# A chunked delta-rule scan and two MoE layers on one core: a rebuilt opening, and the second half backwards

## The chip, the core and the metric

The kernel runs on one core of a Trainium2 chip (trn2). Its time is device time in microseconds, from the first to the last instruction and what lies around them; lower is better. Engines are named as in the profile: PE (TensorE's matmuls) and PEld (its weight loads), DVE (VectorE), ACT (ScalarE), POOL (GpSimd), SP (which only issues DMAs here).

## What is computed

A scan with the delta rule over 768 steps for 4 x 8 heads of 48, a gated MoE layer of 384 by 2048, and a soft-routed MoE layer of 8 experts. Cut to what matters:

```python
# q, k, v: (4, 8, 768, 48) f32, beta: (4, 8, 768)
k_n = k / (norm(k) + 1e-06)
for t in range(768):
    y[t] = q[t] @ state
    state = state + beta[t] * outer(k_n[t], v[t] - k_n[t] @ state)
x = y.reshape(3072, 384)
h = x @ w_in                        # 384 x 2048, w_in and w_out are float64
x = (h * sigmoid(h)) @ w_out        # 2048 x 384
P = exp(x @ w_gate - max)           # 3072 x 8
for _ in range(8):
    P /= P.sum(1) + 1e-09
    P /= P.sum(0) + 1e-09
    P *= 3072 / 8
out = sum(P[:, e:e+1] * (relu(x @ w1[e]) @ w2[e]) for e in range(8))   # 384 x 1024 x 384
```

## The kernel before

Products are made from a high and a low part in fp32r (hh, hl, lh), so every operand is split in two beforehand: high part by ScalarE's copy, low part by a subtraction.

**Phase 1** runs to about 780 us. The scan goes in 12 steps s of 64 positions. Of each step the key grams `gk` (one for each of two batch pairs bp) are multiplied on PE (`gram_k`), negated into `gneg` by ACT, written to DRAM (`nd`), and read back as `nu`, one 32 x 32 matrix on a partition; one `nu` holds two steps, j = s // 2. `tri(j)` inverts it on DVE: a root and scale chain on 128 x 32 values, one multiplication of `nu`, then 31 columns of 118 short operations on `tmpu` and `tu`, and a last multiplication. ACT copies the result to `nu`, which goes through DRAM (`rd`, `td`) into `rt` and `td11`. `merge` joins the halves (z, r), and the chain of a step on PE, ACT and DVE is c (state read), d, y (output) and s (state), t (transposition) and `x1`. For each block of 256 tokens follow, for 8 values of p, h (18 matmuls of 128x256) with the gate g, and x2p (18 matmuls). These are the bulk of PE's work in phase 1. The weights of this layer are float64 in DRAM: `weight()` takes each of 32 tiles of 128x384 to high and low part: ACT takes the absolute value, POOL bounds it (`guard`), DVE makes four passes (L806, L817, L819, L812), ACT copies the high part, and the low part is the residual, for the first `NPE` tiles by PE (`wp`: three matmuls and an ACT copy), for the others by POOL in two operations (L849, L852).

**Phase 2** is two halves m of 1536 tokens with 32 units n each. A unit has 15 products p (three matmuls of 128x512) from weights `wa`, sums by DVE, POOL and ACT (`room`, `h`), and 12 outputs o (six of 128x384) with `wb`, added to `acc`. POOL and ACT prepare `wa` and `wb` of the next unit (`weights`), and `tokens(m)` prepares the tokens of a half.

What order each engine runs in is settled by a list scheduler (`Order`): operations are added with an engine, a cost, dependencies, a priority and pools (`take`), and it emits, by modelled times, the ready one with the highest priority. `IDLE` and `pe()` are part of its model of PE: while PE would wait it fills in dummy matmuls (`idle`). `FIRST` raises the priority of the first step's chain. Costs, priorities and pool sizes are numbers written by hand, so a new number moves rows on every engine.

Of the kernel before, what the change touches and what calls it, by code (L numbers as in the profile page):

```python
# [33 lines left out]
NPE = 13  # L34
IDLE = 30
# [6 lines left out]
FIRST = 2  # L42
# [156 lines left out]
def kernel(  # L199
# [72 lines left out]
    sc = Order({"a": 3, "m": 2, "x": 1, "wy": 3, "sg": 3, "g": 2, "x1": 2, "stg": 4, "wt": 3, "wp": 3, "ke": 2, "gneg": 1,  # L272
# [30 lines left out]
    def load_kv(s, prio):  # L303
# [8 lines left out]
    def load_k(s, bp, prio):  # L312
# [5 lines left out]
        x = op("SP", 0.27, lambda: go(0), prio=prio, take=["ke"])  # L318
        return [x, op("SP", 0.27, lambda: go(1), [(x, -9.0)], prio=prio)]

    def gram_k(s, bp):
# [21 lines left out]
        e = O["gn", s, bp] = op("ACT", 0.48, ev, [m], prio=4.5)
        sc.free(m, "a", [e])
        if bp == 0:
            O["gm", s] = m
            return
        es = [O["gn", s, 0], e]
        j, hf = s // 2, s % 2
        w = []  # L350

        def put(q):
            if q == 0 and hf == 0:
                T["nd", j] = dram.tile([128, 1024], F32, tag="nd", bufs=2, name=f"nd{j}")
            g = T["gneg", s].rearrange("p b h c -> p (b h) c")
            c0, r0 = 32 * (q % 2), 64 * hf + 16 * q
            nc.sync.dma_start(out=T["nd", j][r0:r0 + 16].rearrange("u (r c) -> r u c", c=32),
                              in_=g[32 * q:32 * q + 32, :, c0:c0 + 32])
# [1030 lines left out]
```

## Time and profile before

| | |
|---|---|
| runs, us | 2299.9, 2299.54, 2294.35 (median 2299.54) |
| profiled execution, us | 2295.31, span 2293.5 |
| granted PE clock, mean over the span | 0.976 |
| busy PE, DVE, ACT, POOL | 96%, 77%, 45%, 72% |
| chain that ended last, by engine | PE 77%, DVE 12%, POOL 2% |
| forty slices of 57 us, PE's busy tenths | 6, 6, 7, 8, then 9 to the end |

The shares are averages over stages with different limits. Of the forty slices only the first four are not full on PE, and the granted clock reads 8, 7, 7 and 9 tenths there.

### The profile page before, as it was taken

Reading aid. Unit: us, or ns where it says so; the run is one execution under the profiler, and the core shown is the slowest. Engines: PE = TensorE matmul, PEld = TensorE weight load, DVE = VectorE, ACT = ScalarE, POOL = GpSimd, SP = SyncE. Lnnn points to the kernel's source line nnn. Section 1 sums busy time; section 2 is a strip of 40 time slices with the busy share of each in tenths; the row PEclk is TensorE's granted clock in tenths of the full one; section 3 lists DMA queues with packets and bytes.
Section 4 is the critical chain, followed back from the end, with each engine's and each line's share of the span. In section 5 each row is a group of like instructions: output and inputs, shape, how many; then the busy total and the mean of one; then the engine's idle time right before and its main releaser. Section 6 shows DMA issues by size and latency. Waiting matters only on the chain.

```text
span 2293.5 us, 43638 instructions
## 1 busy us (share of the span) xinstructions
PE 2198.0 (96%) x17378; PEld 2018.9 (88%) x17378; DVE 1767.2 (77%) x2975; ACT 1030.8 (45%) x1794; POOL 1655.5 (72%) x1480
## 2 busy tenths in 40 slices
PE   6678999999999899999999999999999999999999
PEld 5578988999999788999998999988999999999998
DVE  6997777453223788888888888897888888888887
ACT  4433333333334545545454545455445454545453
POOL 5577543433436788898888888897888888888884
PEclk8779999999999999999999999999999999999999
DMA  8523432222102101010101111111111111010101
GB/s 215 150 69 91 100 80 75 66 70 60 45 14 77 70 28 35 28 42 28 42 28 35 35 35 35 35 56 49 35 35 35 35 30 40 28 42 28 42 28 49
DMA packets 121837, 121.78 MB, mean 53 GB/s; under 512 B 82657, under 2 KB 90593, under 8 KB 121633
## 3 DMA queue, kind: packets, MB, share of 16 engines
q1 hardware_dynamic: 121632, 118.99, 18.2%
q8 instruction: 136, 2.23, 0.4%
q14 instruction: 69, 0.56, 0.1%
HBM read 100.09 MB, written 18.87 MB: 52 GB/s over the span
## 4 chain that ended last, share of the span: by engine, by line
PE 77%; DVE 12%; POOL 2%; issue 1%; ACT 1%; DMA 1%; SPq 0%; DVEq 0%; POOLq 0%; ACTq 0%
PE o L1242 33%; PE p L1156 27%; PE h L673 6%; PE x2p L714 6%; DVE tu L488 3%; DVE tmpu L490 2%; DVE s L971 2%; DVE sg L682 1%; DVE room L971 1%; PE d L596 1%; PE y L611 1%; PE c L577 1%; DMA kqp<-in_kq 0%; DVE wr L817 0%; PE s L627 0%
## 5 line engine op out<-in xcount | busy, mean ns | idle before, releaser
L1156 PE MATMUL p<-room,wa 128*128 128x512 f32 x2880 | 738.4, 396 | 4.6 <-DVE s L971 2.8
L1156 PEld LDWEIGHTS p<-room,wa 128*128 128x128 f32 x2880 | 537.0, 188 | 103.9 <-ACT wa L1063 3.2
L1242 PE MATMUL o<-wb,room 128*128 128x384 f32 x2784 | 603.0, 338 | 8.9 <-POOL room L971 3.6
L971 DVE TENSOR_TENSOR s<-s,p 128x512 f32<-128x512 f32 x704 | 476.1, 684 | 154.2 <-ACT s L1170 61.7
L1242 PEld LDWEIGHTS o<-wb,room 128*128 128x128 f32 x2784 | 500.2, 188 | 28.4 <-POOL room L971 4.6
L971 POOL TENSOR_TENSOR room<-s,room 128x512 fp32r<-128x512 f32 x232 | 319.9, 1379 | 226.5 <-ACT s L1189 174.8
L1258 DVE SCALAR_TENSOR_TENSOR acc<-o,pr,acc 128x384 f32<-128x384 f32 x708 | 421.4, 612 | 46.1 <-PE o L1242 42.4
L1242 PE MATMUL o<-wb,h 128*128 128x384 f32 x1824 | 419.3, 338 | 4.5 <-DVE sm L1312 3.1
L1242 PEld LDWEIGHTS o<-wb,h 128*128 128x128 f32 x1824 | 329.2, 188 | 24.3 <-DVE sm L1312 3.7
L971 POOL TENSOR_TENSOR wa<-wraw,wa 128x640 fp32r<-128x640 f32 x192 | 327.8, 1720 | 0.6 <-ACT wa L1063 0.6
L1187 ACT ACTIVATE room<-s 128x512 fp32r<-128x512 f32 x232 | 145.6, 628 | 385.6 <-DVE s L971 385.6
L971 POOL TENSOR_TENSOR wraw<-wraw 128x256 f32<-128x256 f32 (+2 forms) x384 | 280.9, 752 | 15.1 <-DMA wraw<-in_w 5.4
L690 POOL TENSOR_TENSOR g<-sg,g 128x512 fp32r<-128x512 f32 x96 | 128.4, 1338 | 214.6 <-ACT g L686 214.1
L1189 ACT ACTIVATE s<-s 128x512 f32<-128x512 f32 x384 | 243.1, 633 | 12.2
L1063 ACT ACTIVATE wa<-wraw 128x640 fp32r<-128x640 f32 x192 | 140.8, 734 | 234.0 <-POOL wraw L971 223.6
L714 PE MATMUL x2p<-g,w 128*128 128x256 f32 x1728 | 234.9, 291 | 7.5 <-POOL g L690 5.8
L673 PE MATMUL h<-x,w 128*128 128x256 f32 x1728 | 229.4, 289 | 5.5 <-DVE sg L682 5.5
L714 PEld LDWEIGHTS x2p<-g,w 128*128 128x128 f32 x1728 | 218.8, 196 | 12.5 <-POOL g L690 7.2
L971 DVE TENSOR_TENSOR s<-p,s 128x512 f32<-128x512 f32 x320 | 218.9, 684 | 7.2 <-PE p L1156 2.7
L673 PEld LDWEIGHTS h<-x,w 128*128 128x128 f32 x1728 | 216.1, 194 | 8.7 <-DVE sg L682 6.3
L971 POOL TENSOR_TENSOR h<-s,h 128x512 fp32r<-128x512 f32 x152 | 209.0, 1375 | 10.2 <-ACT s L1189 10.0
L971 DVE TENSOR_TENSOR s<-s,s 128x512 f32<-128x512 f32 x192 | 202.7, 1056 | 2.3
(163 smaller groups left out, 2342.2 us busy)
## 6 DMA issues: line engine op xcount, KB each, us to landing
wraw<-in_w SPq DMA_DIRECT2D x128, 384.0 KB, 3.1
kv<-in_kv SPq DMA_DIRECT2D x12, 768.0 KB, 4.9
kqp<-in_kq SPq DMA_DIRECT2D x40, 192.0 KB, 3.5
wr<-in_w_in SPq DMA_DIRECT2D x16, 384.0 KB, 5.3
wr<-in_w_out SPq DMA_DIRECT2D x16, 384.0 KB, 4.4
x2d<-xr SPq DMA_DIRECT2D x36, 128.0 KB, 1.7
xraw<-x2d SPq DMA_DIRECT2D x6, 768.0 KB, 7.5
out<-acc SPq DMA_DIRECT2D x24, 192.0 KB, 1.9
```

Of the source, the lines that this page charges most:

```text
L488: nc.vector.tensor_tensor(out=tu[:, a:b, 0:k], in0=tu[:, a:b, 0:k], in1=tv, op=ALU.add)
L490: nc.vector.tensor_tensor(out=tv, in0=nu[:, a:b, t:k].to_broadcast([128, b - a, k]), in1=tu[:, t:k, 0:k].to_broadcast([128, b - a, k]), op ...
L673: nc.tensor.matmul(out=ps[:, i], lhsT=w[:, k, wl], rhs=x[:, k, xl], start=n == 0, stop=n == 8)
L690: nc.gpsimd.tensor_tensor(out=g[:, 1], in0=T["sg", b, p], in1=f32(g)[:, 0], op=ALU.subtract)
L714: nc.tensor.matmul(out=T["x2p", b][j], lhsT=w[:, wl, 128 * j:128 * j + 128], rhs=g[:, gl, i], start=p == 0 and n == 0, stop=p == NP - 1 an ...
L971: e.tensor_tensor(out=out, in0=in0, in1=in1, op=o)
L1063: nc.scalar.activation(P2[key][:, :, 0], R(3 + 5 * g, 8 + 5 * g), AF.Copy)
L1156: nc.tensor.matmul(out=ps, lhsT=w[:, i, wl], rhs=x[:, xl], start=k == 0, stop=k == 2)
L1187: nc.scalar.activation(P2[key][:, 0], buf(x), AF.Relu)
L1189: op2("ACT", 0.52, lambda: nc.scalar.activation(buf(x), buf(x), AF.Relu), writes=[("s", n, x)], prio=PR_H)
L1242: nc.tensor.matmul(out=ps, lhsT=h[:, hl, 128 * i:128 * i + 128], rhs=w[:, wl], start=c == 0, stop=c == 5)
L1258: op2("DVE", 0.53, lambda A=A, pk=pk, t=t: nc.vector.scalar_tensor_tensor(out=A(), in0=P2[pk], scalar=P2["pr"][:, t, e:e + 1], in1=A(), op ...
```

## The change

In the opening: the key loads, grams and `nd` writes of steps 0 and 1 get priority 30; two loads each of step 1 and some of the reads of `nu` and `rt` are issued by ACT. `nd` is now written per step in its natural layout (two contiguous writes) and `units(j)` reads it into `nu` in eight scattered reads; `gl` is gone. The gram q·k of the first two steps, its mask, the square and reduction of the norms wait for the first inverse or move from POOL to DVE and ACT. `weight()` converts two tiles in one instruction for 24 of the 32 tiles; the guard moves from POOL to DVE, and PE makes all 32 residuals, those from the ninth on in a pool shared with the other matmuls. `NPE`, `IDLE`, `FIRST`, pool sizes and costs are changed. In phase 2 the second half takes its units from the last to the first, so that unit 32 uses unit 31's `wa` and `wb`, and no preparation stands between. By count PE has 57 matmuls of residuals and 57 idle ones more; POOL has 93 fewer operations.

```diff
-NPE = 13
-IDLE = 30
+NPE = 8
+IDLE = 0.9
-FIRST = 2
+FIRST = [20, 5] + [0] * 10
-    sc = Order({"a": 3, "m": 2, "x": 1, "wy": 3, "sg": 3, "g": 2, "x1": 2, "stg": 4, "wt": 3, "wp": 3, "ke": 2, "gneg": 1,
+    sc = Order({"a": 3, "m": 2, "x": 1, "wy": 3, "sg": 3, "g": 2, "x1": 2, "stg": 3, "wl": 2, "wp": 3, "ke": 2, "gneg": 1,
...
         def ev():
+            if s < 2 and bp:
+                nc.vector.tensor_scalar(out=T["gneg", s][:, bp], in0=T["gk", s, bp], scalar1=-1.0, scalar2=None, op0=ALU.mult)
+            else:
...
+        def put():
+            if bp == 0:
+                T["nd", s] = dram.tile([128, 16, CH], F32, name=f"nd{s}")
+            nc.sync.dma_start(out=T["nd", s][:, 8 * bp:8 * bp + 8], in_=T["gneg", s][:, bp])
+    def units(j):
...
+        for s in (2 * j, 2 * j + 1):
+            for q in range(4):
...
+                by = "ACT" if s == 1 and q % 2 else "SP"
...
+                    (nc.scalar if by == "ACT" else nc.sync).dma_start(
+                        out=nu[r0:r0 + 16], in_=T["nd", s][32 * q:32 * q + 32, :, c0:c0 + 32].rearrange("r u c -> u r c"))
...
-        m = op("PE", 1.26, pe, O["ld", s][bp] + ([O["gn", 3, 1]] if s < 2 else []), prio=5, take=["a"], turn=1)
+        m = op("PE", 1.26, pe, O["ld", s][bp] + ([O["td2", 0]] if s < 2 else []), prio=5 if s < 2 or s > 3 else 1.5, take=["a"], turn=1)
-        if s < 2:
-            e = [op("ACT", 0.48, lambda p=p, b=b: nc.scalar.activation(t[p, b], T["gq", s, bp][p], AF.Copy), [m], prio=-8)
-                 for p, b in at]
-            O["pm", s, bp] = [op("POOL", 1.25, lambda p=p, b=b: nc.gpsimd.tensor_tensor(
-                out=t[p, b], in0=t[p, b], in1=mask[p].unsqueeze(1).to_broadcast([64, H, CH]), op=ALU.mult),
-                [x, O["mask"]], prio=5.5) for x, (p, b) in zip(e, at)]
+        e = O["pm", s, bp] = [op("DVE", 0.6, lambda p=p, b=b: ev(p, b), [m, O["mask"]], prio=31) for p, b in at]
...
-    def weight(kind, f):
+    def weight(kind, f, m):
...
-            nc.gpsimd.tensor_scalar(out=T["wm", n], in0=T["wm", n], scalar1=TINY_HI, scalar2=None, op0=ALU.max)
+            v.tensor_scalar(out=t(), in0=t(), scalar1=TINY_HI, scalar2=None, op0=ALU.max)
...
         def rest():
-            ps = T["wp", n] = psX.tile([128, 512], F32, tag=f"x{n % 3}", name=f"wp{n}")[:, 0:DM]
+            if n < NPE:
+                ps = T["wp", n] = psX.tile([128, 512], F32, tag=f"x{n % 3}", name=f"wp{n}")[:, 0:DM]
+            else:
+                ps = T["wp", n] = psA.tile([128, 512], F32, tag="a", name=f"wp{n}")[:, 0:DM]
...
-        def rest_pool():
-            nc.gpsimd.tensor_tensor(out=view(f32(t())), in0=view(f32(hw())), in1=f32(part(0)), op=ALU.subtract)
...
-        def lo_pool():
-            nc.gpsimd.tensor_tensor(out=part(1), in0=view(f32(t())), in1=view(f32(lw())), op=ALU.add)
...
-    keys(0, 13.5)
-    keys(1, 6)
+    keys(0, 30)
+    keys(1, 30)
+    units(0)
...
-            for f in range(2 * p, 2 * p + 2):
-                weight(kind, f)
+            for f in range(2 * p, 2 * p + 2, 2 if p < NP - 2 else 1):
+                weight(kind, f, 2 if p < NP - 2 else 1)
...
+    def wn(n):
...
+        return NQ - 1 if n == NQ else n
...
+    def at(n):
+        return (0, n) if n < NQ else (1, 2 * NQ - 1 - n)
...
     for n in range(2 * NQ + 1):
-        if n + 1 < 2 * NQ:
-            weights((n + 1) % NQ, n + 1)
+        if n + 1 < 2 * NQ and n + 1 != NQ:
+            weights(at(n + 1)[1], n + 1)
```

How rows move, at four places. First VectorE from where it waits for `nu` (L419 and L417 are the same line of the root chain); `wt` and `wr` are tiles of a weight. Before:

```order
L419 TENSOR_SCALAR rta<-nu 128x32
L806 TENSOR_SCALAR wt_342<-wm_311 128x384
L817 SCALAR_TENSOR_TENSOR wr_251<-wr_251,wt_342 128x384
L819 TENSOR_SCALAR wt_342<-wr_251 128x384
L812 SCALAR_TENSOR_TENSOR wl_352<-wr_251,wt_342 128x384
L415 RECIPROCAL rta<-du 128x32
L416 TENSOR_TENSOR rta<-rta 128x32
```

After:

```order
L919 TENSOR_TENSOR wgr<-wgs,wgr 128x3x8
L417 TENSOR_SCALAR rta<-nu 128x32
L413 RECIPROCAL rta<-du 128x32
L414 TENSOR_TENSOR rta<-rta 128x32
L415 TENSOR_TENSOR rta<-rta,du 128x32
L416 TENSOR_SCALAR du<-rta 128x32
```

A whole weight tile stood between the wait and the root chain, and none stands there now. On GpSimd, from the norms of step 1 to the refill of `tu` (L461), which comes behind the first inverse, the order was:

```order
L802 TENSOR_SCALAR wm_523<-wm_523 128x384
L434 TENSOR_TENSOR sq_1_562<-kv_370 128x384
L442 TENSOR_TENSOR kv_370<-kv_370,ne_518 128x384 x2
L401 TENSOR_TENSOR kqp_84<-kqp_84,mask 64x512 x2
L401 TENSOR_TENSOR kqp_85<-kqp_85,mask 64x512 x2
L401 TENSOR_TENSOR kqp_86<-kqp_86,mask 64x512 x2
L401 TENSOR_TENSOR kqp_87<-kqp_87,mask 64x512 x2
```

and now, from the opening's last memsets:

```order
L288 MEMSET kqp_86 32x512
L288 MEMSET kqp_87 32x512
L463 MEMSET tu 128x1024
L464 MEMSET tu 128x32
L443 ISA
L443 TENSOR_TENSOR kv_353<-kv_353,ne_427 128x384
```

The guards, squares and mask multiplications are gone from there; the first `kv` waits for norms that wait for the first inverse. Third, TensorE between the first products and the merge of step 2. Before, at the third and fourth h of the first block (`d` is the scan's):

```order
L714 MATMUL x2p_0_1620<-g_1_1614,w_344 128x256 x6
L714 MATMUL x2p_1_1621<-g_1_1614,w_344 128x256 x6
L714 MATMUL x2p_2_1622<-g_1_1614,w_344 128x256 x6
L673 MATMUL h_2_1721<-x_0_1342,w_882 128x256 x18
L596 MATMUL d_0_1749<-wq_0_1686,rt 64x48 x16
L673 MATMUL h_3_1772<-x_0_1342,w_1031 128x256 x18
```

After, behind the fifth x2p of the first block:

```order
L721 MATMUL x2p_0_1577<-g_4_2077,w_1942 128x256 x6
L721 MATMUL x2p_1_1578<-g_4_2077,w_1942 128x256 x6
L721 MATMUL x2p_2_1579<-g_4_2077,w_1942 128x256 x6
L872 MATMUL wp_2133<-wr_1728,ident 128x384
L873 MATMUL wp_2133<-w_2104,nident 128x384
L874 MATMUL wp_2133<-wl_2043,nident 128x384
L872 MATMUL wp_2139<-wr_1728,ident 128x384
L873 MATMUL wp_2139<-w_2104,nident 128x384
L874 MATMUL wp_2139<-wl_2099,nident 128x384
```

Residuals of weights, three matmuls each, now stand between the products. Last, GpSimd at the turn of the halves. Before:

```order
L971 TENSOR_TENSOR room_10143<-s_9397,room_10143 128x512
L971 TENSOR_TENSOR h_10153<-s_9398,h_10153 128x512
L971 TENSOR_TENSOR wb_10092<-wraw_9384,wb_10092 128x384
L971 TENSOR_TENSOR wb_10096<-wraw_9384,wb_10096 128x384
L971 TENSOR_TENSOR wraw<-wraw 128x256
L971 TENSOR_TENSOR wraw<-wraw 128x128
L971 TENSOR_TENSOR wraw<-wraw 128x256 x2
L971 TENSOR_TENSOR wraw<-wraw 128x384
L971 TENSOR_TENSOR wraw<-wraw 128x256
L971 TENSOR_TENSOR wa_9385<-wraw,wa_9385 128x5x128
L971 TENSOR_TENSOR wa_9386<-wraw,wa_9386 128x5x128
```

After, the corresponding rows (numbers of names are shifted by one):

```order
L984 TENSOR_TENSOR xt_9391<-xraw 128x512
L984 TENSOR_TENSOR h_10157<-s_9397,h_10157 128x512
L984 TENSOR_TENSOR room_10144<-s_9398,room_10144 128x512
L984 TENSOR_TENSOR wb_10093<-wraw_9385,wb_10093 128x384
L984 TENSOR_TENSOR h_10154<-s_9399,h_10154 128x512
L984 TENSOR_TENSOR wb_10097<-wraw_9385,wb_10097 128x384
L984 TENSOR_TENSOR room_10000<-xraw,room_10000 128x512
L984 TENSOR_TENSOR xraw<-xraw 128x512
L984 TENSOR_TENSOR wa_9387<-wraw,wa_9387 128x5x128
```

The second pass over `wraw` with its `wa` between those `wb` and the tokens' `room` and `xraw` is gone.

## Rows read from the trace of the kernel before

**Rows 1.** The page: busy line of all engines; then a line of its DMA issues.

```profile
PE 2198.0 (96%) x17378; PEld 2018.9 (88%) x17378; DVE 1767.2 (77%) x2975; ACT 1030.8 (45%) x1794; POOL 1655.5 (72%) x1480
...
kqp<-in_kq SPq DMA_DIRECT2D x40, 192.0 KB, 3.5
```

**Rows 2.** Windows: stretch, length, busy PE PEld DVE ACT POOL, granted clock, DMA share, GB/s.

```profile
120.00:140.00 20.00, 15.34 (x242) 14.12 (x243) 19.56 (x36) 9.41 (x17) 13.24 (x12) 0.75 0.27 83
140.00:160.00 20.00, 15.33 (x175) 14.46 (x175) 19.64 (x32) 4.94 (x10) 13.99 (x13) 0.76 0.09 14
160.00:300.00 140.00, 131.72 (x1952) 125.11 (x1951) 105.66 (x205) 51.47 (x93) 87.21 (x84) 0.96 0.36 90
```

**Rows 3.** Timeline (start, us, engine, line, operation, idle before): nu and the first inverse.

```profile
25.51 0.34 SPq L380 DMA_DIRECT2D nu<-nd  x1
...
30.21 0.26 DVE L419 TENSOR_SCALAR rta<-nu 128x32 f32<-128x32 f32 x1 [0.80 <-DMA nu<-nd]
...
34.34 1.75 DVE L480 TENSOR_TENSOR nu<-nu,du 128x1024 f32<-128x1024 f32 x1
...
37.34 0.26 DVE L490 TENSOR_TENSOR tmpu<-nu,tu 128x16 f32<-128x16 f32 x2
...
75.94 1.23 DVE L503 TENSOR_TENSOR tu<-tu,du 128x1024 f32<-128x1024 f32 x1
```

**Rows 4.** Timeline: columns of the first inverse on DVE, and GpSimd beside them.

```profile
55.03 1.54 DVE L490 TENSOR_TENSOR tmpu<-nu,tu 128x91 f32<-128x91 f32 x2
...
63.89 1.55 DVE L490 TENSOR_TENSOR tmpu<-nu,tu 128x64 f32<-128x64 f32 x2
...
65.37 0.48 DVE L488 TENSOR_TENSOR tu<-tu,tmpu 128x64 f32<-128x64 f32 x2
...
53.67 11.43 POOL L401 TENSOR_TENSOR kqp<-kqp,mask 64x512 f32<-64x512 f32 x8
```

**Rows 5.** Timeline of PE: from the first merge z to h, and z of step 2.

```profile
87.33 1.53 PE L545 MATMUL z<-rt,td 32*32 32x32 f32 x64 [0.45 <-DMA rt<-rd]
...
101.46 0.42 PE L611 MATMUL y<-xs,kqp 112*64 112x48 f32 x2 [4.35 <-ACT xs L601]
...
114.41 0.31 PE L611 MATMUL y<-xs,kqp 112*64 112x48 f32 x1 [5.27 <-DVE xs L632]
...
122.38 0.90 PE L644 MATMUL t<-ident,y 128*128 128x128 f32 x3 [4.57 <-ACT y L616]
...
125.06 4.34 PE L673 MATMUL h<-x,w 128*128 128x256 f32 x18
...
209.12 1.20 PE L545 MATMUL z<-rt,td 32*32 32x32 f32 x64
```

**Rows 6.** Timeline of PE: a residual, a key gram, and one h.

```profile
88.80 0.94 PE L841 MATMUL wp<-wr,ident 128*128 128x384 f32 x2
...
90.02 0.27 PE L332 MATMUL gk<-ke 48*64 48x64 f32 x1
...
91.09 0.94 PE L841 MATMUL wp<-wr,ident 128*128 128x384 f32 x2
...
233.82 2.42 PE L673 MATMUL h<-x,w 128*128 128x256 f32 x18
```

**Rows 7.** Timeline of DVE: the first operations of two successive weight tiles.

```profile
77.09 0.35 DVE L806 TENSOR_SCALAR wt<-wm 128x384 int32<-128x384 int32 x1
...
79.01 0.35 DVE L806 TENSOR_SCALAR wt<-wm 128x384 int32<-128x384 int32 x1
```

**Rows 8.** Groups by line and shape, POOL, 80 to 300 us.

```profile
L849 POOL TENSOR_TENSOR wt<-wr,w 128x384 f32<-128x384 f32 x19 | 21.2, 1117 | 10.4 <-ACT w L836 8.2 <-ACT sg L678 2.2
```

**Rows 9.** Windows of a middle stretch and the turn; POOL's groups, 1515 to 1562 us.

```profile
1000.00:1200.00 200.00, 200.00 (x1012) 182.09 (x1011) 173.15 (x270) 97.03 (x165) 169.06 (x147) 1.00 0.11 34
1520.00:1540.00 20.00, 14.93 (x72) 12.36 (x72) 19.72 (x26) 11.87 (x21) 19.84 (x17) 0.99 0.23 80
1540.00:1560.00 20.00, 16.42 (x71) 13.69 (x72) 18.03 (x25) 8.16 (x14) 18.80 (x14) 0.92 0.28 98
...
L971 POOL TENSOR_TENSOR wa<-wraw,wa 128x640 fp32r<-128x640 f32 x6 | 10.2, 1712 | 0.0
```

More of the change, by code (lines that the diff above doesn't have):

```diff
@@ L122, in pe @@
     def pe(self, t, cost, cols):
+        slow = 2 if cols > 768 or cols == 256 else 1.5
         left = 1.0
@@ L126, in pe @@
             k = int(t / self.TICK + 1e-6)
-            c = cost if self.cols.get(k - 1, 0) >= self.FULL else 2 * cost
+            c = cost if self.cols.get(k - 1, 0) >= self.FULL else slow * cost
             x = min(left, ((k + 1) * self.TICK - t) / c)
@@ L298, in load_part @@
         t = kqp[(2 * s + bp) % 4]
-        after = [(O["nl", 0], -1.0), O["z", 2 * s + bp]] if part else []
+        after = [(x, -1.0) for x in O["nl", 0]] + [O["z", 2 * s + bp]] if part else []
+        if s and not part:
+            return [(op("ACT", 0.45, adma(t[64:112, 0], kq[s, bp, 0, :, 0]), prio=prio), 2.3),
+                    (op("ACT", 0.45, adma(t[0:48, 0], kq[s, bp, 1, :, 0]), prio=prio), 2.3)]
         return [op("SP", 0.27, dma(t[64:112, part], kq[s, bp, 0, :, part]), after, prio=prio),
@@ L347, in gram_k @@
             return
[L348 to L358, printed above, removed]
@@ L858, in weight @@
-        a = op("SP", 1.09, ld, free, prio=-9 if n >= 3 else 9.2, take=[] if n < 2 * NF - 1 else ["x1"])
-        ab = O["wabs", n] = op("ACT", 0.41, absolute, [a], prio=-4, take=["stg"])
-        x = op("POOL", 1.14, guard, [ab], prio=-3.5)
-        xs_ = []
-        for c, fn in parts:
-            take = ["wt"] if fn is shift else ["sg"] if fn is tail and n < NPE else []
-            x = op("DVE", c, fn, [(x, 0.13)], prio=1.5, take=take, turn=0)
-            xs_.append(x)
-        sc.free(ab, "stg", [xs_[0]])
@@ L867, in weight @@
-        before = [O["whi", n - 1], O["wlo", n - 1]] if n else []
-        h = O["whi", n] = op("ACT", 0.41, hi, [xs_[1]] + before, prio=7.5)
-        if n < NPE:
-            sc.free(xs_[0], "wt", [x])
-            x = op("PE", 0.97, rest, [x, h, O["ident"], O["nident"]], prio=11, take=["wp"], turn=0, cols=1536)
-            sc.free(xs_[3], "sg", [x])
-            l = op("ACT", 0.41, lo, [x], prio=19.5)
-            sc.free(x, "wp", [l])
+        if p == NP - 1:
+            before = [O["whi", n - 1], O["wlo", n - 1]]
+        elif i:
+            before = [(O["whi", n - 1], 0.0)]
+        else:
+            before = [O["wlo", m] for m in range(max(0, n - 4), n)]
```

230 lines of the change are left out of this document (124 added, 106 removed).

## The prediction

> **What bounds the kernel now.** I first read the busy shares and the forty slices. TensorE is busy 96% of the span [rows 1], and its slices read 9 from the fifth on: away from the start the kernel is bound by TensorE's matmuls, and only a stretch in which TensorE stands, or runs at a low granted clock, can give time back. So I went on with the windows of 20 us. The start is such a stretch: from 120 to 160 us TensorE is busy 15.3 of each 20 us at a granted clock of 0.75, while VectorE is busy 19.6 [rows 2]. Busy share times clock is what TensorE did of what it could: 0.58 there, 0.90 from 160 to 300 (131.72 of 140 at 0.96). I call this the yield. The only other one that the change touches is the turn from the first half of the products to the second, at 1520 to 1560, below.
>
> The timeline of the start then shows who is waited for. The matrix nu, on which the first inverse works, was issued at 25.51 and VectorE waited for it until 30.21; the multiplication that follows stands at 34.34, the first column of the inverse at 37.34, and its last multiplication ends at 77.2 [rows 3]. Behind it come ScalarE's copy, rd, rt and the first merge z at 87.33, and from there one long serial chain, in which TensorE waits 4.35, 5.27 and 4.57 us for results of ScalarE and VectorE, to the first product h at 125.06 [rows 5]. Only from there is there bulk work.
>
> **The change part by part.**
>
> *Keys first.* Loads, key grams, evictions, nd and nu now stand at the head of their queues. A key load takes 3.5 us to land [rows 1], nu took 4.7 us from issue to its first reader [rows 3]. Issue at 1.2, keys of the second step some 2 us later on ScalarE's queue: landed by 6.9; four grams at 1.07 us [rows 6] while others arrive, 10; eviction 0.6; nd written at a load's 3.5, 14.1; nu at 4.7, 18.8. The eight scattered reads in place of one contiguous one are not shown before; at 0.36 us of issue for six in a row on SP I add 0.7: 19.5. Bounds: 17 (evictions overlap) and 24 (the 1.6 MB of weights issued ahead of nd, and the two conversions that stand before nu on VectorE, come in between).
>
> *GpSimd still.* From the root to the first column VectorE took 7.1 us (30.21 to 37.34), in which one weight tile and the norms' reductions lie; by the order these are gone, 4.0 remain. The columns took 38.6 us (37.34 to 75.94). While GpSimd made its eight mask multiplications (53.67, 11.43 us), a pair of 128x91 took 1.54 us; a pair of 128x64 took 1.55 while they ran and 0.48 right behind them [rows 4]. In the new order GpSimd has nothing but memsets until the inverse is through. From 65.37 to 75.94, with GpSimd still, 58 of the 118 column operations took 10.57 us [rows 3, 4]; at that rate all take an estimated 21.5. With the last multiplication of 1.2: end at 19.5 + 4.0 + 21.5 + 1.2 = 46.2, where it was 77.2.
>
> The Trainium skill (SBUF — State Buffer, "Who interferes with whom") has a reason for these rows: a VectorE instruction with two inputs in SBUF and a GpSimd one that reads SBUF lock each other out for a whole instruction. Rows 4 agree in which operations stretch. The rule also speaks against the change: pairs of weight tiles make VectorE's instructions nearly twice as long, and GpSimd's halves of g, some fourteen until the third merge, would each wait up to 0.5 us more (a tile's 1.92 us over four passes); that estimate, 7 us, stands in no term of the sum.
>
> *First chains favoured.* From the inverse's end to z were 10.1 us (77.2 to 87.33), to h a further 37.7. Half of the latter is conversions placed between, and two of three waits are for results that VectorE or ScalarE made late. Behind the inverse the new order gives VectorE fifty rows before h: some 24 us of work, with four mask pairs and nearly four pairs of tiles among it. So h comes 24 to 26 us behind the inverse, if rt lands as before: 46 + 25 = 71 (bounds 65 and 80) in place of 125.
>
> *Weights two at a time, all residuals on TensorE.* This is not free: 19 tiles more get their low word from TensorE at 1.22 us each (88.80 to 90.02 [rows 6]), 23 us of new work. It is in the following count. What it saves is GpSimd's: 19 times 1.1 us [rows 8], twice, and the guards, which go to VectorE. VectorE's 1.92 us for a tile [rows 7] becomes about the same with the guard (one more operation, but four fixed costs halved): nothing either way.
>
> *The count to the third merge.* From h to the z of step 2, the new order of TensorE holds 15 h and 12 x2p of 18 matmuls each (2.42 us, both 128x256 [rows 6]): 65.3; 28 residuals, 34.2; 10 key grams, 10.7; 18 short pieces of the scan at about 1 us, 18. Together 128 us. At a yield of 0.58 (120 to 160 before) this takes 221 us, at 0.90 142, at 0.95 135. I take 0.92, so 139: TensorE has about twice the work of before in this stretch, VectorE less than before, and GpSimd's conversions are gone. The end is at 71 + 139 = 210, where z of step 2 was at 209.1 [rows 5]. At that point the new kernel is ahead, by the two orders, by 12 key grams, 3 h and 5 x2p: 12.8 + 19.4 = 32 us that TensorE, the bound of everything after, need not do later. Opening: 32 - 1 = **31 us** gained, 36 at a yield of 0.95, 10 at 0.80.
>
> *Second half backwards.* Its first unit is the last of the first half, so its weights are there and one unit's preparation on GpSimd falls away, with its loads. At the turn TensorE is busy 14.93 of 20 us at 0.99 and then 16.42 at 0.92, where it is busy 200 of 200 elsewhere: 14.8 and 15.1 of 20, so some 10 us lost. GpSimd is full there, 19.84 and 18.80; the first pass over wa alone is 5.1 us for a unit (six for two units, 10.2) [rows 9], and wb and wraw come on top. But VectorE is at 19.72 as well, with the new tokens. I take 7 of the 10; bounds 0 and 10. What is late next is VectorE's s and room.
>
> The rest (Sqrt table early, Square on ScalarE, put_low gone, 57 more idle matmuls, which fill holes before the first z) has its cover: ScalarE is busy 45% and the idle matmuls stand ahead of waits. I cost it at nothing; without cover the idle ones are 57 x 0.13 = 7 us, in the first 45 us only.
>
> **Sum.** The profiled execution is 2295.3 us: 2295.3 - 31 - 7 = 2257. The median of three runs (2299.5) lies 4.2 above it, so 2261 against the runs (the forecast).
>
> **The rivals.**
>
> 1. *The conversion throttles the products.* A tile passes VectorE, ScalarE, TensorE and ScalarE again, with two buffers for the low words and three for the pairs, and each product of the first token block waits for its tile. With the yield at 0.78 the stretch takes 164 us, the opening gains 6 us, the time is 2287. For: VectorE was full from 120 to 160 [rows 2]. Against: TensorE gets other blocks' h and key grams in between.
>
> 2. *Slower: TensorE starves and its clock stays down.* The same place, the mechanism that the rows from 120 to 160 show already: TensorE waits for a full VectorE, its busy share sinks, the granted clock is 0.75, and everything takes longer. Now 34 us of residuals lie in that stretch, which it didn't hold before. It decides below a yield of 0.72 (128/0.72 = 178; 71 + 178 = 249, about 209 + 32 + 7). At 0.65 it is 2320, at the 0.58 of before 2343. Against: the ratio of TensorE's work to VectorE's is much higher than it was there.
>
> 3. *The turn doesn't gain.* VectorE at 19.72 of 20 is the real bound there, and a still GpSimd changes nothing, so the change doesn't do there what it says: 2269.
>
> 4. *More.* Rows of 1.22 us for a residual and 2.42 for a product contain pieces at a low clock and overlapping; if the true work is a tenth less (13 us) and done at 0.95, the opening gives 49, the turn 10: 2240.
>
> **How the numbers follow.** Forecast (yield 0.83 to 0.95, turn 3 to 10): 0.55, 2253 to 2281. Rival 1: 0.20, a quarter of it within 0.3% of no change. Rival 2: 0.09, some 0.02 of it within 0.3%. Rival 3: 0.10. Rival 4: 0.06. A measurement can tell about 0.3% (7 us) from no change. Faster: 0.55 + 0.15 + 0.10 + 0.06 = 0.86; same 0.05 + 0.02 = 0.07; slower 0.07. The range leaves out half of rival 4 and the slow end of rivals 1 and 2: 2238 to 2292. Predicted is the forecast, 2261.
>
> **What would show it.** In the profile after: nu lands at 17 to 24; the column pairs of the first inverse take under 0.6 us all through; its last multiplication ends at 43 to 50; first h at 65 to 80; the windows from there to the third merge show TensorE's busy share times clock near 0.9; z of step 2 at 200 to 225; the turn shows no weight preparation on GpSimd and less idle on TensorE. I am wrong if the inverse still ends behind 60 (nu late, or its operations stretched by something else than GpSimd), if the yield behind h is that of 120 to 160 before, or if phases between 300 and 1500, which the change hardly touches, get longer and give the lead back.

## The result, and the profile after

The changed kernel takes 2311.21 us (median of 4 runs, 2308.43 to 2312.69) where the kernel before, in the runs beside it, takes 2298.09 (2294.35 to 2299.9): ratio 1.0055, 95% interval 1.004 to 1.0069. It is some 13 us slower; 2261 was predicted, and 2292 was the upper end of the range. The profiled execution is 2310.37 us with a span of 2308.6, 15.1 more than the 2293.5 of before.

The page's busy line, to be set beside [rows 1]:

```profile
PE 2223.4 (96%) x17506; PEld 2036.2 (88%) x17506; DVE 1746.3 (76%) x2971; ACT 1030.6 (45%) x1792; POOL 1543.7 (67%) x1387
```

GpSimd lost 112 us of work, as meant. TensorE got 25 us more: the residuals that had been GpSimd's low words, and the new idle matmuls. It is still busy 96%.

**The start.** The timeline of the kernel after (start, length, engine, line, operation, idle time before it and what ended it), to be set beside [rows 3 to 5]:

```profile
25.07 0.19 DVE L417 TENSOR_SCALAR rta<-nu 128x32 f32<-128x32 f32 x1 [5.19 <-DMA ke<-in_kq]
...
28.78 0.27 DVE L493 TENSOR_TENSOR tmpu<-nu,tu 128x16 f32<-128x16 f32 x2
...
36.11 0.47 DVE L493 TENSOR_TENSOR tmpu<-nu,tu 128x91 f32<-128x91 f32 x2
...
49.47 1.23 DVE L506 TENSOR_TENSOR tu<-tu,du 128x1024 f32<-128x1024 f32 x1
...
65.78 1.92 PE L552 MATMUL z<-rt,td 32*32 32x32 f32 x64 [4.84 <-DMA rt<-rd]
...
85.75 3.54 PE L680 MATMUL h<-x,w 128*128 128x256 f32 x18
...
231.24 1.51 PE L552 MATMUL z<-rt,td 32*32 32x32 f32 x64
```

The first inverse ends at 50.7 where it ended at 77.2, and the first product starts at 85.75 where it started at 125.06. Up to there the kernel is 39 us ahead. But the merge of step 2, at 231.24, is 22 us behind the 209.12 of before. The reads of nu and VectorE between 164 and 224 show why:

```profile
164.40 3.50 SPq L384 DMA_DIRECT2D nu<-nd  x4
...
177.71 0.19 DVE L417 TENSOR_SCALAR rta<-nu 128x32 f32<-128x32 f32 x1 [6.77 <-DMA nu<-nd]
180.78 1.22 DVE L483 TENSOR_TENSOR nu<-nu,du 128x1024 f32<-128x1024 f32 x1
...
220.83 1.22 DVE L506 TENSOR_TENSOR tu<-tu,du 128x1024 f32<-128x1024 f32 x1
```

This is the second inverse, on which the merges of steps 2 and 3 wait. Its nu was read only from 164.40 on, its columns start behind 180.78, and it ends at 222.1; before, it ended at 197.5.

**Where it was lost.** Windows of the kernel after (columns as in [rows 2]), in the stretches of [rows 2], then from 160 to 200, then the two in which the lead goes:

```profile
120.00:140.00 20.00, 19.58 (x265) 16.07 (x265) 16.29 (x28) 10.63 (x20) 1.67 (x1) 1.00 0.20 58
140.00:160.00 20.00, 20.00 (x253) 16.69 (x250) 12.45 (x25) 13.12 (x28) 2.57 (x2) 1.00 0.50 165
160.00:300.00 140.00, 121.85 (x1462) 112.28 (x1459) 96.02 (x215) 48.21 (x90) 49.30 (x48) 0.90 0.27 64
...
160.00:200.00 40.00, 31.29 (x244) 26.95 (x240) 25.02 (x62) 18.16 (x35) 5.35 (x4) 0.87 0.35 93
...
240.00:300.00 60.00, 55.02 (x860) 51.53 (x860) 48.43 (x100) 16.50 (x33) 32.81 (x33) 0.91 0.20 50
300.00:500.00 200.00, 183.60 (x2734) 174.05 (x2733) 133.43 (x272) 65.11 (x116) 97.16 (x96) 0.97 0.34 68
```

The last two of them in the kernel before:

```profile
240.00:300.00 60.00, 57.52 (x940) 54.30 (x939) 43.32 (x94) 20.97 (x38) 29.65 (x31) 0.97 0.36 88
300.00:500.00 200.00, 190.58 (x2968) 181.50 (x2965) 134.63 (x274) 68.80 (x125) 85.48 (x87) 0.98 0.31 78
```

From 120 to 160 all is as was hoped: yield 0.99 instead of 0.58. From 160 on it is worse than before: 0.68 from 160 to 200, and busy time times clock from 240 to 500 is 228 us (50.1 and 178.1) against 243 (55.8 and 186.8). By the same product, summed over windows of 10 us, TensorE did 190 us of work up to 240 where it had done 154; about 30 of these 36 are no lead, since 23 are the new residuals and some 7 the new idle matmuls.

Over the whole span the same sum says what the change came to. TensorE's work rose from 2158 to 2188 us, and what it lost by standing or by a low clock fell from 136 to 120: the change bought 15 us of lost time with 30 us of work, of which the idle matmuls only fill holes. For the forecast, some 38 us less span, the lost time would have had to fall to about 67.

The lead of 39 us was gone already at the end of the first token block. Its eighth and last h, which needs the last weights of `w_in`, starts where it started before (timeline; first before, then after):

```profile
190.03 2.42 PE L673 MATMUL h<-x,w 128*128 128x256 f32 x18
```

```profile
190.42 4.47 PE L680 MATMUL h<-x,w 128*128 128x256 f32 x36
```

So the products of this block went at the pace of the weights' conversion, which ends at 210 in both kernels, and what TensorE did more by then was other work.

The merges z of steps 4 and 11 tell the rest (timeline; first before, then after, each with the last multiplication of the third inverse):

```profile
259.55 1.23 DVE L503 TENSOR_TENSOR tu<-tu,du 128x1024 f32<-128x1024 f32 x1
...
300.74 1.20 PE L545 MATMUL z<-rt,td 32*32 32x32 f32 x64
...
659.02 1.20 PE L545 MATMUL z<-rt,td 32*32 32x32 f32 x64
```

```profile
298.57 1.23 DVE L506 TENSOR_TENSOR tu<-tu,du 128x1024 f32<-128x1024 f32 x1
...
309.65 1.29 PE L552 MATMUL z<-rt,td 32*32 32x32 f32 x64 [0.71 <-DMA rt<-rd]
...
669.20 1.20 PE L552 MATMUL z<-rt,td 32*32 32x32 f32 x64
```

The third inverse, which uses the same buffer nu as the second, comes 39 us later than before, and now z of step 4 follows 10 us behind it and waited for its rt; before, 40 us lay between. Step 4 is 8.9 us behind, step 11 10.2, and from step 11 to the end the kernel takes 1639.4 us instead of 1634.5. Those last 4.9 us lie mostly in the start of the second phase. In all kernels below this remainder is between 1634 and 1643 us; why is left open.

**The turn** (windows after, to be set beside [rows 9]):

```profile
1520.00:1540.00 20.00, 19.81 (x100) 17.70 (x99) 19.31 (x31) 10.54 (x19) 19.84 (x17) 1.00 0.08 21
1540.00:1560.00 20.00, 13.22 (x57) 11.14 (x58) 19.93 (x23) 7.79 (x15) 14.13 (x10) 0.86 0.24 79
```

The kernel after is some 13 us late here, so the two slices do not hold the same work as in [rows 9]. A wider window holds the whole turn (first before, then after):

```profile
1490.00:1600.00 110.00, 101.35 (x489) 89.79 (x488) 92.11 (x133) 60.15 (x105) 97.06 (x79) 0.97 0.17 55
```

```profile
1490.00:1600.00 110.00, 101.19 (x496) 90.18 (x495) 93.73 (x134) 61.46 (x109) 85.42 (x70) 0.97 0.14 44
```

GpSimd has 12 us less to do, the weights' preparation, but TensorE is idle as long, 8.8 us and 8.7 before, and VectorE is full in the two slices.

### The profile page after: what moved, and what is told of

The parts are those of the page before. It is cut to its first block, busy times and chain, and to the rows that moved or that the text cites. A ratio compares the mean times of both kernels' runs of the same rounds, so it can differ in the third digit from the quotient of the medians.

```text
span 2308.6 us, 43774 instructions
## 1 busy us (share of the span) xinstructions
PE 2223.4 (96%) x17506; PEld 2036.2 (88%) x17506; DVE 1746.3 (76%) x2971; ACT 1030.6 (45%) x1792; POOL 1543.7 (67%) x1387
## 4 chain that ended last, share of the span: by engine, by line
PE 70%; DVE 11%; POOL 8%; DMA 5%; issue 3%; ACT 2%; SPq 1%; DVEq 0%; POOLq 0%; ACTq 0%
PE o L1260 28%; PE p L1173 23%; PE h L680 6%; PE x2p L721 6%; DVE s L984 3%; POOL room L984 2%; DVE tmpu L493 2%; DVE tu L491 2%; POOL wa L984 1%; DMA kqp<-in_kq 1%; POOL wraw L984 1%; POOL h L984 1%; DVE acc L1276 1%; DMA rt<-rd 1%; DVE room L984 1%
## 5 line engine op out<-in xcount | busy, mean ns | idle before, releaser
L984 POOL TENSOR_TENSOR wa<-wraw,wa 128x640 fp32r<-128x640 f32 x189 | 321.6, 1714 | 2.1 <-ACT wa L1076 2.1
L984 POOL TENSOR_TENSOR wraw<-wraw 128x256 f32<-128x256 f32 x378 | 274.2, 746 | 15.5 <-DMA wraw<-in_w 5.7
L984 DVE TENSOR_TENSOR s<-s,s 128x512 f32<-128x512 f32 x192 | 212.9, 1109 | 2.3
```

What stands on the lines that cost most here:

```text
L984: e.tensor_tensor(out=out, in0=in0, in1=in1, op=o)
```

## The experiments

Two theories stood at first. **A**: the second inverse comes late since its grams are made last, and the third merge waits for it. **B**: the weights' conversion, longer by the residuals on TensorE, is what throttles. A third came from the first runs. **E**: both end at nearly the same time, and each hides what the other one gains. The table collects what the traces show, in us; "inverse 2" is the end of the second inverse, "last weight" the end of the last write of a weight's low word, by ScalarE or GpSimd, z4 and z11 the merges of steps 4 and 11. The span is that of the one profiled execution; the ratio is that of all runs to runs of the kernel before beside them.

| kernel | inverse 2 | last weight | z4 | z11 | span | ratio to before (95%) |
|---|---|---|---|---|---|---|
| before | 197.5 | 209.8 | 300.7 | 659.0 | 2293.5 | |
| after | 222.1 | 210.2 | 309.7 | 669.2 | 2308.6 | 1.0055 (1.004 to 1.0069) |
| e1 steps 2, 3 first | 146.9 | 241.0 | 315.2 | 667.3 | 2307.4 | 1.0071 (1.0056 to 1.0085) |
| e2 residuals on GpSimd | 245.5 | 212.6 | 332.5 | 699.3 | 2337.3 | 1.0158 (1.0137 to 1.018) |
| e3 both | 155.3 | 229.8 | 309.0 | 672.9 | 2312.2 | 1.0073 (1.0056 to 1.009) |
| e5 residuals early | 250.2 | 191.4 | 328.2 | 690.3 | 2332.0 | 1.013 (1.0113 to 1.0147) |
| e6 single tiles | 216.3 | 204.4 | 298.7 | 666.1 | 2306.6 | 1.0019 (1.0007 to 1.0031) |
| e7 no residuals | 227.9 | 160.1 | 307.3 | 667.1 | 2302.2 | 1.0038 (1.0027 to 1.005) |
| e8 three orders | 147.5 | 218.3 | 312.3 | 674.5 | 2311.1 | 1.0062 (1.0047 to 1.0077) |
| e9 e1 and e7 | 158.9 | 186.0 | 274.7 | 637.2 | 2271.8 | 0.9883 (0.987 to 0.9896) |
| e10 e1 and e6 | 155.8 | 222.0 | 286.7 | 652.6 | 2288.2 | 0.9978 (0.9967 to 0.9989) |

**e1: the grams of steps 2 and 3 first** (after, with one edit).

```diff
-    keys(2, 2)
-    keys(3, 2)
+    keys(2, 7)
+    keys(3, 7)
```

> The changed kernel with one number changed twice: the key loads of steps 2 and 3 get priority 7 in place of 2, so they stand ahead of those of steps 4 to 11 (priority 6). Theory A (the second inverse started late because its grams were made last): its nu is read at about 65 to 80 us and not at 164, its last multiplication ends before 180 us (222 in the changed kernel), z of step 2 is before 200 (231), and the time falls by 25 to 45 us to 2266 to 2286. Theory B (the weight conversion with all residuals on TensorE is what holds the opening back): the inverse moves, but TensorE still waits on residuals and VectorE on low-word buffers, and the time stays within 8 us of the changed kernel, 2303 to 2312.

The second inverse ended 75 us earlier, and nothing was gained:

```profile
145.66 1.23 DVE L506 TENSOR_TENSOR tu<-tu,du 128x1024 f32<-128x1024 f32 x1
...
240.50 0.49 ACT L877 ACTIVATE w<-wp 128x384 fp32r<-128x384 f32 x1 [0.71 <-PE wp L874]
...
315.15 1.39 PE L552 MATMUL z<-rt,td 32*32 32x32 f32 x64 [1.15 <-DMA rt<-rd]
```

The last weight came 31 us later instead: VectorE makes both, and the inverse now ran among the passes over the tiles. Step 4 came 5.5 us later too. That the late grams make the late inverse is shown; that they alone make the kernel slow is refuted.

What held the kernel instead stands in TensorE's order. By kernel.py the update d of step 2 waits for the eighth h of the first block, and this h for the tiles of `w_in`. Here z of step 2 is at 156.47, and d stands right behind that h all the same:

```profile
209.75 2.31 PE L680 MATMUL h<-x,w 128*128 128x256 f32 x18
212.00 1.13 PE L603 MATMUL d<-wq,rt 64*64 64x48 f32 x32
```

**e2: the residuals of tiles 13 to 31 on GpSimd again** (pairs of tiles kept), and **e3**: e1 and e2.

```diff
+RES = 13
...
+        if n >= RES:
+            x = op("POOL", 1.12, lambda: nc.gpsimd.tensor_tensor(
+                out=view(tw()), in0=view(f32(word())), in1=f32(part(0)), op=ALU.subtract), [xs_[-1], h], prio=1)
+            x = op("POOL", 1.12, lambda: nc.gpsimd.tensor_tensor(
+                out=part(1), in0=view(tw()), in1=view(f32(low())), op=ALU.add), [x], prio=9.5)
```

> The changed kernel with the residuals of tiles 13 to 31 on GpSimd in two operations, as before, and nothing else. Theory A: the second inverse still gets its nu after 150 us, so TensorE is not the bound there and the 19 tiles less give under 8 us: 2303 to 2312. Theory B: 19 tiles at 1.0 to 1.2 us and the waits for low-word buffers (15 us on VectorE) fall away, 17 to 25 us: 2286 to 2294.

> Both of the two edits: steps 2 and 3 first, and tiles 13 to 31 on GpSimd. Theory A: as with steps 2 and 3 first alone, 2266 to 2286, and less by up to 17 us if TensorE is then the bound from the first product on, so down to 2250. Theory B: about as with the residuals on GpSimd alone.

Neither theory's range held, in either run. e2 made things worse (2332.8): its last weight comes no earlier, its second inverse 23 us later. e3 is no better than after (2314.46). Putting the residuals back where they were is no cure.

**e5: residuals early on TensorE**, and **e8**: e5's edit, e1's, and priority 1 in place of 11 for VectorE's reduction of the norms of steps 2 and 3.

```diff
-        x = op("PE", 0.97, rest, [xs_[-1], h, O["ident"], O["nident"]], prio=4 if n < 4 else 1.9, take=[kind_], turn=0, cols=1536)
+        x = op("PE", 0.97, rest, [xs_[-1], h, O["ident"], O["nident"]], prio=4 if n < 4 else 12, take=[kind_], turn=0, cols=1536)
```

> The changed kernel with the priority of the residual matmuls of tiles 4 to 31 at 12 in place of 1.9, so that TensorE's order has them ahead of key grams and products. Theory C (VectorE is the bound of the opening, and stands 52 of the 150 us from 50 to 200 because it waits in its own order, 15 us of it for low-word buffers that residuals behind other matmuls on TensorE hold): VectorE's waits for residuals fall from 15 to under 5 us, the last weight is written by 200 (210), 2298 to 2306. Rival D (TensorE's work counts, and its order doesn't): 2308 to 2315.

> The changed kernel with three changes of order: steps 2 and 3 first, residuals at priority 12, and the sums of squares of steps 2 and 3 at priority 1 in place of 11 (VectorE waited 9.5 us for one). Theory C: VectorE's idle time between 50 and 200 us falls from 52 to under 30, the last weight is written before 215 and the third merge before 170, and the time falls to 2285 to 2300. Rival D: 2308 to 2315.

e5 has its last weight 19 us earlier and its second inverse 28 later, its first h at 141.1 instead of 85.75, and is 17 (by the ratios) to 20 us (by the medians) slower than after, outside both ranges. The two bounds trade against each other. e8 has both moderately early (147.5 and 218.3), but its first h is at 159.9, and it stays where after is (2314.52), as rival D had it.

**e6: tiles one by one again.**

```diff
-            for f in range(2 * p, 2 * p + 2, 2 if p < NP - 2 else 1):
-                weight(kind, f, 2 if p < NP - 2 else 1)
+            for f in range(2 * p, 2 * p + 2):
+                weight(kind, f, 1)
```

> The changed kernel with every tile converted by itself as before, residuals still all on TensorE. If the pairs help, as the fixed costs say: VectorE has 24 x 4 x 0.15 / 2 = 7 us more work, time 2311 to 2320. If the pairs hold a buffer and the low words longer and so cause the waits (Theory C): VectorE's waits for residuals fall and the time with them, 2298 to 2307.

VectorE's waits from 50 to 200 us (engine, line, waited for, us in total, times, the longest), after and e6:

```profile
DVE wl L843 <- PE wp L874: 15.1, 15, 4.9
DVE ne L448 <- POOL sq L435: 9.7, 2, 9.5
DVE rta L417 <- DMA nu<-nd: 6.8, 1, 6.8
DVE rta L413 <- ACT ne L419: 6.6, 2, 5.3
```

```profile
DVE wl L843 <- PE wp L874: 6.1, 7, 2.6
```

In the kernel after, VectorE's low word wl waits 15 times for a residual to give back one of two buffers; with single tiles it waits 6.1 us in place of 15.1, and the kernel is 6.5 us (by the medians) to 8 us (by the ratios) faster than after. The plan differs in more than the tiles: it has 112 idle matmuls in place of 183, all of them before 56 us, and its first h comes no earlier (89.56). That the pairs cost something, in a place where the prediction had "nothing either way", is likely and not shown by this run alone.

**e7: no residuals for tiles 8 to 31** (their low words are zero; VectorE's tail and TensorE's three matmuls are left out), and **e9**: e7 and e1.

```diff
+        if n >= NPE:
+            l = op("ACT", 0.45, lambda: nc.scalar.activation(part(1), view(f32(word())), AF.Copy, scale=0.0), [xs_[-1], h], prio=19.5)
```

> The changed kernel without the residuals of tiles 8 to 31: their low parts are set to zero by a copy, VectorE's low-word operation and TensorE's three matmuls are left out. Theory C: VectorE loses 24 x 0.56 = 13 us of work and the waits for residuals (15 us), and the last weight is ready 25 us earlier, but the second inverse still gets its nu behind the key grams of steps 4 to 11; TensorE loses 24 to 29 us of work. 2282 to 2295. Rival D (only TensorE's work counts): 2282 to 2287. If the second inverse alone sets the end: 2303 to 2311.

> The changed kernel with steps 2 and 3 first and without the residuals of tiles 8 to 31 (low parts zero): the two edits that gave nothing each. Theory E (two bounds of about the same length hold the opening, the second inverse and the weight conversion, and each hides the other): with both gone the second inverse ends by 160 us and the last weight is written by 200, the merge of step 4 comes before 275 (309.6 in the changed kernel), and the time falls to 2255 to 2285. If neither bounds the end (Theory F: TensorE and the scan's pace of 51 us a step set it, whatever the opening does): 2300 to 2312.

e7, window and timeline:

```profile
200.00:240.00 40.00, 4.79 (x77) 4.29 (x77) 25.77 (x69) 3.63 (x5) 3.19 (x5) 0.54 0.23 46
...
236.14 0.28 PE L552 MATMUL z<-rt,td 32*32 32x32 f32 x2 [31.49 <-issue]
```

The weights are done at 160 and TensorE runs through all it can do; then it stands 31.49 us, to z of step 2, which starts 8 us behind the end of the second inverse; the granted clock of the window is 0.54. So some 30 us of TensorE's work and 50 us of conversion less gave 6 us of span. e1 alone gave 1 us of span and e7 alone 6, and by the medians of all runs neither gave anything (2311.79 and 2310.62 beside 2311.21); e9, both, gave 37 us of span, 40 by the medians:

```profile
157.64 1.22 DVE L506 TENSOR_TENSOR tu<-tu,du 128x1024 f32<-128x1024 f32 x1
...
185.43 0.54 ACT L889 ACTIVATE w<-wr 128x384 fp32r<-128x384 f32 x1
...
274.67 1.20 PE L552 MATMUL z<-rt,td 32*32 32x32 f32 x64
...
637.17 1.20 PE L552 MATMUL z<-rt,td 32*32 32x32 f32 x64
```

This is as theory E said, each hiding what the other costs. But much of it is work left out. By busy time times clock, in windows of 10 us over the whole span:

| kernel | TensorE's work, us | lost, us | span |
|---|---|---|---|
| before | 2158 | 136 | 2293.5 |
| after | 2188 | 120 | 2308.6 |
| e1 | 2189 | 118 | 2307.4 |
| e7 | 2158 | 145 | 2302.2 |
| e9 | 2159 | 113 | 2271.8 |

From e7 to e9 the work is the same and 32 us of lost time go: the late second inverse costs them, once the weights are early. From e1 to e9, 30 of the 36 us are work that TensorE no longer does, and 5 are lost time. So e9 shows that the late inverse hides the price of the residuals. It does not show the conversion as a second bound apart from TensorE's own work, and it is no proof that the kernel could reach 2271 with all its work.

**e10: e1 and e6 together**, all work kept.

> The changed kernel with tiles converted one at a time and steps 2 and 3 first, all work kept. Theory E: the second inverse ends by 160 us; the conversion, which single tiles made 6 us shorter, ends between 210 and 235, and is then the only bound: 2295 to 2308. Theory F: 2302 to 2312.

```profile
154.59 1.22 DVE L506 TENSOR_TENSOR tu<-tu,du 128x1024 f32<-128x1024 f32 x1
...
286.68 1.20 PE L552 MATMUL z<-rt,td 32*32 32x32 f32 x64
...
652.60 1.20 PE L552 MATMUL z<-rt,td 32*32 32x32 f32 x64
```

2292.64 us where its before took 2296.88: faster than both kernels, by 4 us than before and, by the two ratios, by 18 than after. Step 4 is at 286.7, 14 us before that of before. This is better than either theory's range. Against e1 the last weight is 19 us earlier; the eighth h starts at 194.58 and d of step 2 at 196.82, each 15 us earlier, and the span is 19 us shorter. From 60 us on TensorE's work is the same in both (2138 and 2140 us), so 17 of the 19 us are lost time. This is the run that speaks for the conversion as the second bound. It is one plan beside another, though, and e11 below shows how far plans can differ.

**e12 to e14: more for e10**. e12 gives the residuals of tiles 20 to 31 to GpSimd, e13 its guards, and e14 sets the residuals' priority to 3.5 (it was 1.9).

```diff
-        x = op("DVE", 0.35 * m - 0.12 * (m - 1), guard, [first], prio=1.4)
+        x = op("POOL", 1.14, guard, [first], prio=-3.5)
```

> The run with single tiles and steps 2 and 3 first (2292.6), and the residuals of the last twelve tiles on GpSimd in two operations. If TensorE's queue holds the conversion back (VectorE waits 4.9 us for residuals there, and TensorE does 12 x 1.2 = 14 us of them): the last weight is written before 215 us (222), 2278 to 2290. If VectorE is what holds it, GpSimd's 24 operations beside it stretch its own: last weight after 222, 2292 to 2302.

> The same run with the guard on GpSimd again, one pass of five less on VectorE for each tile (32 x 0.36 = 11.5 us). If VectorE's own work holds the conversion: last weight by 213 us, 2280 to 2289. If waits in its order hold it: the step to GpSimd and back adds one, 2292 to 2302.

> The same run with residuals at priority 3.5 on TensorE in place of 1.9 (12 made the changed kernel 20 us slower, since the first product came at 141 us). If the residuals' place in TensorE's order is what costs: last weight by 213 us, first product still before 95, 2280 to 2290. Else 2292 to 2310.

Ratios 1.0006 (0.9992 to 1.0021), 1.0026 (1.0013 to 1.0039) and 1.0041 (1.0026 to 1.0056), all worse than e10's; each time ends at or just above the higher range expected. The last weight was written at 222.2, 230.2 and 227.5, e10's at 222.0. None of these levers shortens the conversion; what would is open. e12 says one thing more: its second inverse ends at 158.8 and its last weight at 222.2, both within 3 us of e10, and yet its step 4 is at 296.5 and its span 2299.8, 12 us longer. The two milestones do not set the time alone; what else does is open.

**e4: the turn alone** (before, with the second half backwards).

```diff
+    def at(n):
+        return (0, n) if n < NQ else (1, 2 * NQ - 1 - n)
...
-        if n + 1 < 2 * NQ:
-            weights((n + 1) % NQ, n + 1)
+        if n + 1 < 2 * NQ and n + 1 != NQ:
+            weights(at(n + 1)[1], n + 1)
```

> The kernel before with nothing but the second half of the products taken backwards. Forecast of the prediction: 7 us less (3 to 10), so 2288 to 2295 against 2298. Rival 3 (VectorE is the bound at the turn): within 3 us of before, 2295 to 2301, TensorE idle as long between 1520 and 1560 though GpSimd does one preparation less.

2296.17 beside 2296.85: ratio 1.0003 (0.9992 to 1.0015). Windows and one line of the timeline:

```profile
1520.00:1540.00 20.00, 16.85 (x81) 14.08 (x79) 19.76 (x26) 11.13 (x20) 18.25 (x14) 1.00 0.19 63
1540.00:1560.00 20.00, 15.94 (x69) 14.57 (x70) 19.26 (x28) 6.04 (x10) 8.63 (x6) 0.83 0.27 89
1490.00:1600.00 110.00, 102.11 (x501) 91.55 (x500) 93.97 (x134) 57.75 (x101) 86.20 (x69) 0.97 0.15 47
...
1544.06 1.62 PE L1160 MATMUL p<-room,wa 128*128 128x512 f32 x3 [5.50 <-DVE s L971]
```

GpSimd falls from 18.80 of 20 to 8.63, and from 1490 to 1600 TensorE still stands 7.9 us (8.7 before), of which 5.50 at once for VectorE's s.

**e11: the masks alone** (before, with the masks of the first two steps moved from GpSimd to VectorE, behind the first inverse).

```diff
-        m = op("PE", 1.26, pe, O["ld", s][bp] + ([O["gn", 3, 1]] if s < 2 else []), prio=5, take=["a"], turn=1)
+        m = op("PE", 1.26, pe, O["ld", s][bp] + ([O["td2", 0]] if s < 2 else []), prio=5, take=["a"], turn=1)
```

> The kernel before with one part of the change alone: the masks of the first two steps are multiplied by VectorE behind the first inverse, not by GpSimd during it. VectorE is full from 30 to 200 us in the kernel before. Theory E (VectorE's work up to about 200 us bounds the opening there): the first inverse's columns take 22 to 30 us in place of 38.6, VectorE saves some 11 us net, all that follows comes earlier by 8 to 12, and the time falls to 2284 to 2294. Theory F: within 4 us of before.

The first inverse ended at 67.3, 9.9 us earlier, yet the merge of step 1 came at 128.85 (106.32 before) and the kernel took 2310.59, ratio 1.0051 (1.0039 to 1.0063). The columns took 29.5 us (36.54 to 66.08) in place of 38.6, as expected, and both ranges of time were missed. The planner put the rest in another order, and what cost the time is open: the longest waits of VectorE for grams gq, 8.0 and 4.3 us at 178.99 and 204.63, are for masks of later steps, which it made before as well. Of the price of the masks alone this run says little; that a few moved operations shift the whole by 14 us it does say.

## Why the prediction was wrong, point by point

- **GpSimd still: right.** The columns took 20.7 us (28.78 to 49.47) where 21.5 were worked out and 38.6 were needed before; a pair of 128x91 takes 0.47 us in place of 1.54 [rows 4]. Not all of the 18 us is the masks': e11, which moves them alone, saves 9; guards and squares on GpSimd and the norms' operations on VectorE left the columns as well. Root to first column: 3.7 us, 4.0 predicted. The 7 us that the prediction feared for GpSimd's halves of g did not show: they take 1326 ns each up to the third merge, 1329 before.
- **nu: mis-sized.** 25.07 in place of 19.5, above the bound of 24. The last of the four key grams was evicted by VectorE at 14.38 to 15.06, behind passes over the first weights, where 10.6 was reckoned; its nd write stood behind four reads of nu in SP's queue and was issued at 16.77, and the last reads of nu at 20.30. VectorE waited 5.19 us for them. (The profile names a key load, issued behind those reads, which the root chain does not need; the same wait in e6, 4.38 us, it puts down to nu.) The end of the inverse is therefore 50.7 and not 46.2.
- **rt and first h: mis-sized.** From the inverse's end to z took 15 us, not 10 ("if rt lands as before"): z waited 4.84 us for rt, while from 40 to 60 us the DMA engines were busy 0.93 of the time at 323 GB/s. From z to h it took 20 us where 15 were left for it. h at 85.75, not 71; outside the bounds of 65 and 80.
- **The count: right; the yield: mis-sized.** From the first h to the z of step 2, the groups of the trace hold what was counted:

```profile
L680 PE MATMUL h<-x,w 128*128 128x256 f32 x270 | 35.9, 291 | 0.8 <-DVE sg L689 0.8
L721 PE MATMUL x2p<-g,w 128*128 128x256 f32 x216 | 33.4, 314 | 8.5 <-ACT g L693 7.4 <-POOL g L697 1.0
L872 PE MATMUL wp<-wr,ident 128*128 128x384 f32 x56 | 25.7, 541 | 0.0
L347 PE MATMUL gk<-ke 48*64 48x64 f32 x160 | 11.1, 221 | 0.0
```

 15 h and 12 x2p (270 and 216 by 18), 28 residuals (56 by 2) and 10 grams. TensorE was busy 130.45 us there, 128 were counted. But the stretch took 145.5 us, at a busy share times clock of 0.82 (130.45 of 145.49 at 0.92), where 0.92 was taken; the 128 us were summed from rows that hold some time at a lower clock already, so 128/145.5 = 0.88 is what answers to the prediction's use. The third merge: 231 instead of 210, 15 us from the late h and 6 from the yield.
- **The step that failed** is "32 us ahead that TensorE, the bound of everything after, need not do later". It has two faults. First, work made ahead is a lead only while TensorE is what everything waits for. In the stretch to step 4 it was not: z of step 2 stands behind the second inverse, z of step 4 behind the third, which follows the second, and when the inverse is early (e1), the scan stands behind the first block's last h and its weights. In all five kernels with a late second inverse (after, e2, e5, e6, e7) z of step 4 comes 8 to 13 us behind the end of the third; in before and in every other kernel of these runs 30 us or more lie between. The 12 grams, 3 h and 5 x2p made earlier are then missing as filling, which is argued and not measured apart: by the prediction's own count the kernel is 10 us ahead at the third merge (32 less 22) and 8.9 behind at step 4. Second, the prediction looked only at how many grams are made ahead, and not at whose. In the order of the changed kernel, the rows of SP's queue read, with their numbers,

```
24 L358 DMA nd_413<-gneg_303 128x512 x2
...
91 L358 DMA nd_2205<-gneg_2158 128x512
93 L384 DMA nu<-nd_2205 16x32x32 x4
95 L358 DMA nd_2315<-gneg_2250 128x512 x2
96 L384 DMA nu<-nd_2315 16x32x32 x4
```

 nd_413 is of a later step than 2 or 3 and stands 67 rows ahead of those two; nd_2205 and nd_2315, which the second inverse's nu reads, are the last of all. The key loads of steps 2 and 3 had priority 2, so every other step passed them in the two buffers for keys. This could be read before the run.
- **Residuals on TensorE: counted and sized right, not cheap all the same.** 28 of them kept TensorE busy 35.07 us up to the third merge, 34.2 were counted. They are real extra work on the bound engine: with e1's order, leaving out 24 of them and their tail on VectorE gives 36 us of span (e9 against e1, 2307.4 to 2271.8), 30 of them TensorE's work.
- **Pairs of tiles "nothing either way": most likely wrong.** Single tiles give 6.5 us by the medians (2304.72 to 2311.21), and 19 with e1's order (e10 against e1). In the kernel after VectorE is idle 52 of 150 us (50 to 200) and busy 98, where it was busy 143.6 before: it is no longer full, it waits.
- **The turn: rival 3 was right**, 0 in place of 7 (e4). That VectorE is at 19.72 was in the prediction's own rows.
- **The rivals.** Rival 1 named the conversion, and TensorE's order in e1, and e10, bear it out as one half; rival 2's low clock did not come where it was put (1.00 from 120 to 160), and its point of decision, 0.72, was not reached, and the kernel is slower all the same. The last line, that phases between 300 and 1500 "give the lead back", was the right kind of warning, a little too late in its place: most of it happened from 231 to 310.

So the sum's error against the profiled execution is 2310.4 - 2257 = 53: 7 for the turn, 21 for the late third merge, 19 for the lead given back by step 4, 1 to step 11, and 5 behind it.

## What to carry to other kernels

A lead in the order of a queue is worth something only if it is made of what is waited for next: for each serial chain of the opening, look up where its inputs stand in the new order, not how much stands ahead of it. When two chains end within a few us, each alone can give nothing; take away the one, the other, and both (here 1, 6 and 37 us of span) before an edit is called useless, and take off what is only work left out (here some 30 of the 37). And in a planned order every edit reshuffles the rest by some 14 us, so an experiment on one part has to be read by its milestones, not by its total alone.

## What the runs showed of the hardware

Only one thing of size: the same column pair on VectorE took 1.54 us beside GpSimd's mask multiplications and 0.47 without them, in the kernel after and also in e11, which moves the masks alone. The columns together took 38.6, 20.7 and 29.5 us, for other reasons too. The Trainium skill (SBUF — State Buffer, "Who interferes with whom") says that a VectorE instruction with two inputs in SBUF and a GpSimd instruction that reads SBUF contend for a shared port; the trace agrees.
